# The loads of two weight matrices move from the ScalarE and SyncE queues to GpSimd's queue

## The chip, the cores and the metric

The kernel runs on one core of one Trainium2 chip. Time is device time of that core in microseconds (us); a time of the kernel is the median of several runs. The core has TensorE (PE, with its weight loads shown as PEld), VectorE (DVE), ScalarE (ACT), GpSimd (POOL) and SyncE (SP). Each engine runs its own program in order. A DMA command stands in the program of an engine like any other instruction: if it has to wait for a free buffer, what stands behind it on that engine waits too.

## The reference

Block-sparse attention (4 batches, 8 heads, 768 positions, head size 64, blocks of 32) and, on its output, two matrix products with a nonlinearity between them:

```python
scores = scale * q @ k.T                       # per batch and head, masked to a window of 3 blocks,
attn = softmax(where(mask, scores, -1e9))      # 2 global blocks and 3 sampled blocks per row of blocks;
x = (attn @ v) as [3072, 512]                  # first and last row of blocks are dense
h = x @ w_in                                   # w_in  [512, 2048]
g = h * tanh(softplus(h))
out = g @ w_out                                # w_out [2048, 512]
```

## The kernel before

**Staging.** The inputs q, k, v are scaled and split into two half-precision parts, and so are the two weight matrices, so that each product is three half-precision products. Attention runs in jobs: each batch has 13, eleven with two rows of blocks and two dense ones. A job is scores (S, line 661), a maximum on VectorE, exponentials on ScalarE, transposes (T, line 667), the product with v (O, line 789), a normalisation and one more transpose (tx). The second part runs in stages of 256 positions, three to a batch (0, 1, 2): first product h (line 1049, in runs of 12 matmuls), copies hs, elementwise us and g on three engines, second product y (line 1114, in runs of 6 matmuls). The names h_1_5 and y_0_0 give the stage and then the piece of h (0 to 7) or the half of y.

**Weights.** w_in comes in 8 pieces of 1 MB (tile wr, 3 buffers), w_out in 16 pieces of 512 KB (tile wor, in the ring of 6 buffers "raw" that q, k and v use as well). A piece is a wide number; VectorE decodes it in three steps (lines 873, 876, 879). TensorE then forms a Gram matrix of each (gram_wi, gram_wo), from whose diagonal comes one scale: tp_wo (line 387) is the matmul that sums the diagonal for the whole of w_out, so it needs all 16 decoded pieces. After it each piece of w_out is scaled (wt_o, line 965 or 963), rounded (line 969 or 968) and the rest subtracted on GpSimd (line 970). A run of y for two pieces needs those two.

**GpSimd's other work.** The gathers of sampled key blocks (lines 567 and 598, three copies for a row of blocks, six for a job; a few of the first jobs may run on ScalarE), which write one of two buffers kg and so wait for the scores of an earlier job; the low halves of some inputs (lines 507, 522), squares (line 1083) and the low half of g (line 1099).

**What sets the order.** All work is entered as tasks with an engine (or a choice of engines), a duration, what it reads and writes, and a key. A planner, Plan.emit, simulates the engines, picks the task that can start first by its durations (keys and the tables URGE, JOBS and PIECES decide between near ones), and writes the programs in that order. One duration or engine that changes can thus move any task behind it. Where the simulation sees a gap on TensorE between 14 and 200 us of its own time, `fill` writes dummy matmuls into it (line 1309, one for each 0.14 us of the gap; they write an unused part of a bank). Work on the second part is taken when nothing of attention is ready, with the earliest piece first; four buffers g hold its results, so h can run at most about two stages ahead of y.

Of the kernel before, what the change touches and what calls it, by code (L numbers as in the profile page):

```python
# [37 lines left out]
def place(w):  # L38

    name, *at = w[0] if w and isinstance(w[0], tuple) else (None,)  # L40
    if name in ("s", "mx", "nb", "p", "t", "ph", "pl", "o", "r", "tx", "xhw", "xw"):
        return (name, at[0], None) if at[0] < len(JOBS) else (None, None, None)
    if name in ("wr", "wi", "wq", "ws", "wor", "wo"):
        return name, None, at[0] + 8 * (name in ("wor", "wo"))
    if name in ("wd", "wh", "wl", "wt", "dg") and at[0] in ("i", "o") and len(at) > 1:
        return name + at[0], None, at[1] + 8 * (at[0] == "o")
    if name == "gram" and at[0] == "wi":
        return "gram", None, at[1]
    if name in ("raw", "ss", "sc", "hi", "tp", "gram", "ends") and len(at) > 1 and at[1] == 0 or \
            name in ("k", "q", "v", "vd", "kt") and at[0] == 0:  # L50
        return name + str(at[0] if name in ("raw", "ss", "sc", "hi", "tp", "gram", "ends") else ""), None, None
    return (name if name in ("us", "hs", "gh", "gp", "hsw", "kg", "kw", "vg", "ys", "iv", "am") else None), None, None
# [12 lines left out]
class Plan:  # L65
# [10 lines left out]
    def add(self, eng, dur, fn, r=(), w=(), new=(), use=(), key=0.0, lat=0.0, kind=None, port=False, also=()):  # L76

        kind_, i, k = place(w)  # L80
        key += URGE.get(kind_, 0.0) + (JOBS[i] if i is not None else 0.0) + (PIECES[k] if k is not None else 0.0)
        t = Task({eng: (dur, fn, port or (eng == "POOL" and dur)), **{e: (d, f, o) for e, d, f, o in also}}, key, lat,
                 new, kind, len(self.tasks))
        self.tasks.append(t)
        for ring, k in new:
            self.first[k], self.users[k] = t, []
        for k in r:
            t.deps.update(self.writer.get(k, ()))
            self.readers.setdefault(k, []).append(t)
        for k in w:  # L90
            t.deps.update(self.writer.get(k, ()))
            t.deps.update(self.readers.pop(k, ()))
            self.writer[k] = [t]
        for k in {*r, *w, *use}:
            if k in self.users:
                self.users[k].append(t)
                t.deps.add(self.first[k])
        t.deps.discard(t)
        return t
# [109 lines left out]
def attn_mish_kernel(ctx: ExitStack, tc: tile.TileContext, qT, kT, v, sampled, blocks, w_in, w_out, out):  # L209
# [11 lines left out]
    nc = tc.nc  # L221
# [20 lines left out]
    wide = w_in.dtype != F32  # L242
# [12 lines left out]
    wo = const.tile([P, NFC, 2, DM], F16, name="wo")  # L255
# [72 lines left out]
    BOTH = True  # L328
# [3 lines left out]
    add = plan.add  # L332
# [525 lines left out]
    def load_w(pool, key, tag, w, a0, eng):  # L858

        if not wide:  # L860
            eng.dma_start(out=a0, in_=w)
            return
        n = w.free_size()
        raw = new(pool, tag, key, [P, RAW if tag == "raw" else n])[:, 0:n].bitcast(I32)
        eng.dma_start(out=raw.rearrange("p (c f) -> p c f", c=w.shape[1]) if len(w.shape) == 3 else raw, in_=w)
        tl[key] = raw.rearrange("p (f two) -> p f two", two=2)
# [18 lines left out]
    def a0_i(k):  # L885
        return wi[:, k].rearrange("p m t c f -> p (m t c f)").bitcast(F32)

    def load_i(k):
        W = 2 if wide else 1
        src = w_in.rearrange("(c p) f -> p c f", p=P)[:, :, k * 2 * P * W:(k + 1) * 2 * P * W]  # L890
        key, raw = ("wi", k), ("wr", k)

        after = [("raw", "v", 0, 1)]
        if wide:
            go = lambda eng: load_w(pools["w"], raw, "wr", src, None, eng)
            add("ACT", 0.45, lambda: go(nc.scalar), r=after, w=[raw], new=[("wr", raw)], key=-9, lat=2.0,
                kind=("dma", 3.9), also=[("SP", 0.5, lambda: go(nc.sync), False)] if BOTH else ())
            return
        add("ACT", 0.45, lambda: load_w(None, None, None, src, a0_i(k).rearrange("p (c f) -> p c f", c=NCC),
                                          nc.scalar), r=after,  # L900
            w=[key], key=-9, lat=2.0, kind=("dma", 1.95))

    def piece_i(k, cls):

        k0 = k - k % 2
        key, ks, ksc, kp = ("wi", k), ("wq", k0), ("ws", k0), ("tp", "w", k0)
        load_i(k)
        add_decode(("wr", k), key, lambda: a0_i(k), 1.24, cls)

        def ss():  # L910
            if k == k0:
                new(sb, "wq", ks, [P, 2])
            return tl[ks][:, k - k0:k - k0 + 1]
        add_gram(("wi", k), [lambda: a0_i(k)], [key], "h", ss, [ks], [("wq", ks)] if k == k0 else (), cls)
        if k > k0:

            add_root(kp, lambda: tl[ks], lambda: root(kp, new(sb, "ws", ksc, [P, 2]), iv_i[:, k0:k + 1]),
                     [ks], [], [ksc, ("iv", k0)], [("ws", ksc)], cls, apart=True)
            split_i(k0, cls)
            split_i(k, cls)  # L920
# [59 lines left out]
    def a0_o(fc):  # L980
        return wo[:, fc].rearrange("p t d -> p (t d)").bitcast(F32)

    def load_o(fc, after=()):
        raw = ("wor", fc)
        go = lambda eng: load_w(sb, raw, "raw", w_out.rearrange("(c p) f -> p c f", p=P)[:, fc], a0_o(fc), eng)
        add("ACT", 0.45, lambda: go(nc.scalar), r=after, w=[raw] + ([] if wide else [("wo", fc)]), new=[("raw", raw)],
            key=-5, lat=2.0, kind=("dma", 1.95), also=[("SP", 0.5, lambda: go(nc.sync), False)] if BOTH else ())

    def piece_o(fc, cls):

# [182 lines left out]
    for j in T3:  # L1173
        load(0, "v", [j], "us" if j < 2 else "hs")
    add("ACT", 1.0, lambda: which(new), w=["off", "z"],
        new=[("hs", ("z",))], key=-9, lat=6.0)
# [21 lines left out]
    for k in range(NFP):  # L1198
# [3 lines left out]
        key=-9)  # L1202
# [23 lines left out]
    for i, job in enumerate(jobs):  # L1226
# [19 lines left out]
        if i == 1:  # L1246
            LOADO, ATO, ATP = [("dec", 6)], -2.0, -22.0
            for fc in range(NFC):
                load_o(fc, after=LOADO)
                piece_o(fc, ATO)  # L1250
            scale_o(ATO)
            for fc in range(NFC):
                parts_o(fc, ATP)
# [104 lines left out]
```

## Time and profile before

| | |
|---|---|
| median of 3 runs | 789.8 us (788.79 to 790.77) |
| span of the profiled execution, first to last instruction | 786.6 us (the page gives no other time for it; 3.2 under the median) |
| TensorE busy | 740.5 us |
| ScalarE, VectorE, GpSimd busy | 542.7, 493.5, 307.6 us |
| mean granted TensorE clock | 0.990 |
| DMA moved | 95.31 MB, mean 121 GB/s |

In the rows of the profile an engine's work is given as line, engine, operation, output<-input, shape and count, with start and duration or with busy time and mean. "[6.40 <-DMA vg<-vd]" behind a row says that the engine stood idle for 6.40 us before it and what ended that, inferred from semaphores. ACTq, SPq and POOLq are an engine's commands that are not counted as busy, the DMA commands among them. A row with "x8: 374/374/520, 10.5 to 50.9" gives the count, the shortest, median and longest duration in ns, and the start of the first and last.

### The profile page before, as it was taken

Reading aid. Unit: us, or ns where it says so; the run is one execution under the profiler, and the core shown is the slowest. Engines: PE = TensorE matmul, PEld = TensorE weight load, DVE = VectorE, ACT = ScalarE, POOL = GpSimd, SP = SyncE. Lnnn points to the kernel's source line nnn. Section 1 sums busy time; section 2 is a strip of 40 time slices with the busy share of each in tenths; the row PEclk is TensorE's granted clock in tenths of the full one; section 3 lists DMA queues with packets and bytes.
Section 4 is the critical chain, followed back from the end, with each engine's and each line's share of the span. In section 5 each row is a group of like instructions: output and inputs, shape, how many; then the busy total and the mean of one; then the engine's idle time right before and its main releaser. Section 6 shows DMA issues by size and latency. Waiting matters only on the chain.

```text
span 786.6 us, 30628 instructions
## 1 busy us (share of the span) xinstructions
PE 740.5 (94%) x12793; PEld 518.7 (66%) x12793; DVE 493.5 (63%) x900; ACT 542.7 (69%) x880; POOL 307.6 (39%) x393
## 2 busy tenths in 40 slices
PE   6677899888999999999999999999999999999997
PEld 5544578665577767767776676677677667666663
DVE  6868988998767764795866457656665453223220
ACT  3555778768868877777887768786876666455650
POOL 2114244887635542374443422534641331213021
PEclk9989999999999999999999999999999999999999
DMA  9878857104534475244346603523444112000000
GB/s 339 263 236 256 268 176 202 44 2 136 159 117 131 119 198 171 69 162 120 87 139 194 192 15 101 174 77 91 119 115 119 37 39 81 14 15 14 14 14 27
DMA packets 57742, 95.31 MB, mean 121 GB/s; under 512 B 8323, under 2 KB 20612, under 8 KB 57604
## 3 DMA queue, kind: packets, MB, share of 16 engines
q1 hardware_dynamic: 52032, 80.51, 34.9%
q10 hardware_dynamic: 5572, 12.85, 4.8%
q8 instruction: 100, 1.64, 0.9%
q14 instruction: 38, 0.31, 0.1%
HBM read 80.38 MB, written 12.95 MB: 119 GB/s over the span
## 4 chain that ended last, share of the span: by engine, by line
PE 73%; DVE 10%; ACT 6%; DMA 5%; issue 2%; POOL 1%; SPq 1%; POOLq 1%; ACTq 0%; DVEq 0%
PE h_None L1049 27%; PE y L1114 26%; PE obank L789 6%; PE t L667 6%; PE s L661 4%; DMA vg<-vd 3%; PE tx L667 1%; PE wd_i L947 1%; DVE wt_o L965 1%; DMA wr<-in_moe_w_in_dram 1%; DVE hs_None L1087 1%; DVE v L491 1%; DMA raw_k<-in_k_dram 1%; ACT us_None L1078 1%; POOL kt L522 1%
## 5 line engine op out<-in xcount | busy, mean ns | idle before, releaser
L1049 PE MATMUL h_None<-xh,wi 128*128 128x256 f16 x1536 | 282.8, 273 | 0.0
L1114 PE MATMUL y<-wo,g 128*128 128x512 f16 x1152 | 278.0, 380 | 4.0 <-POOL wo L970 2.6
L1049 PEld LDWEIGHTS <-wi 128*128 128x128 f16 x2304 | 223.5, 98 | 47.3 <-issue 2.1
L1049 PE MATMUL h_None<-xl,wi 128*128 128x256 f16 x768 | 209.8, 273 | 0.0
L1114 PEld LDWEIGHTS <-g 128*128 128x128 f16 x1152 | 111.1, 98 | 106.7 <-issue 7.3
L1099 POOL TENSOR_TENSOR g<-hs_None,g 128x1024 f16<-128x1024 f32 x48 | 107.6, 2241 | 188.4 <-DVE g L1096 144.8
L598 POOL COPY kg<-kt 128x256 f16 x258 | 107.2, 451 | 123.3 <-PE s L661 109.7
L1060 ACT ACTIVATE hs_None<-h_None,gsc 128x512 f32<-128x512 f32 x96 | 65.5, 684 | 80.2 <-PE h_None L1049 79.4
L727 ACT ACTIVATE pt<-s,nb,ns 128x256 f32<-128x256 f32 (+1 forms) x208 | 106.3, 582 | 5.7 <-PE t L667 5.0
L750 ACT ACTIVATE ph<-t 128x512 f16<-128x512 f32 x112 | 66.5, 596 | 45.1 <-PE t L667 45.0
L754 DVE SCALAR_TENSOR_TENSOR pl<-t,ph 128x512 f16<-128x512 f32 x105 | 71.9, 686 | 35.8 <-ACT ph L750 35.5
L1087 DVE SCALAR_TENSOR_TENSOR hs_None<-us_None,hs_None 128x1024 f32<-128x1024 f32 x48 | 65.0, 1355 | 40.1 <-ACT us_None L1086 40.1
L667 PE MATMUL t<-ident,pt 128*128 128x128 f32 x448 | 70.4, 280 | 6.8 <-DVE pl L754 3.6
L708 DVE TENSOR_REDUCE mx<-s 128x4 f32<-128x1024 f32 x44 | 53.7, 1222 | 31.9 <-PE s L661 31.3
L1083 POOL TENSOR_TENSOR us_None<-us_None 128x1024 f32<-128x1024 f32 x22 | 44.2, 2007 | 71.8 <-DVE us_None L1081 68.7
L667 PEld LDWEIGHTS t<-ident,pt 128*128 128x128 f32 x448 | 51.6, 142 | 21.4 <-DVE pl L754 4.5
L789 PEld LDWEIGHTS <-ph 128*32 128x32 f16 x3584 | 47.9, 94 | 20.9 <-issue 13.1
L1078 ACT ACTIVATE us_None<-hs_None,hsc 128x1024 f32<-128x1024 f32 x48 | 55.2, 1150 | 0.9
L789 PE MATMUL obank<-vg,ph 128*32 128x65 f16 (+1 forms) x3200 | 50.6, 196 | 4.0 <-DMA vg<-vd 2.2
L1081 DVE TENSOR_SCALAR us_None<-us_None 128x1024 f32<-128x1024 f32 x48 | 37.4, 778 | 25.4 <-ACT us_None L1078 25.2
L1085 ACT ACTIVATE us_None<-us_None 128x1024 f32<-128x1024 f32 x48 | 50.7, 1056 | 1.6 <-POOL us_None L1083 0.8
L1086 ACT ACTIVATE us_None<-us_None 128x1024 f32<-128x1024 f32 x48 | 50.7, 1056 | 0.8
(199 smaller groups left out, 893.6 us busy)
## 6 DMA issues: line engine op xcount, KB each, us to landing
vg<-vd SPq DMA_DIRECT2D x320, 65.0 KB, 2.6
vg<-vd SPq DMA_DIRECT2D x80, 195.0 KB, 3.2
wr<-in_moe_w_in_dram ACTq DMA_DIRECT2D x8, 1024.0 KB, 7.4
vd<-v SPq DMA_DIRECT2D x12, 520.0 KB, 3.8
vg<-vd SPq DMA_DIRECT2D x12, 520.0 KB, 5.1
raw_k<-in_k_dram SPq DMA_DIRECT2D x12, 512.0 KB, 5.4
raw_q<-in_q_dram SPq DMA_DIRECT2D x12, 512.0 KB, 4.3
raw_v<-in_v_dram SPq DMA_DIRECT2D x12, 512.0 KB, 5.0
```

What stands on the lines that cost most here:

```text
L598: nc.gpsimd.tensor_copy(out=dst, in_=tl["kt", b][:, :, ds(j, BS)])
L667: nc.tensor.matmul(out, src, ident, start=start, stop=stop, is_transpose=True)
L727: ex = lambda o, x, g, w: nc.scalar.activation(out=o, in_=x, func=AF.Exp, bias=nb[:, g, w:w + 1], scale=tl["ns", b, sus[w]["qb"] // TB][:, ...
L750: nc.scalar.activation(out=new(sb, "ph", ("ph", i, j), [P, 2, 2, P], F16), in_=tl["t", i, j], func=AF.Copy, scale=PSC)
L754: nc.vector.scalar_tensor_tensor(out=new(sb, "pl", ("pl", i, j), [P, 2, 2, P], F16), in0=tl["t", i, j], scalar=PSC, in1=tl["ph", i, j], op ...
L789: nc.tensor.matmul(o[cs, w, g, 0:v1 - v0], p[:, k, g, cs], vt[:, k, 2 * c + g, v0:v1], start=j == 0 and g == 0 and k == 0 and n == 0, stop ...
L1049: nc.tensor.matmul(h[:, f2, 0:n].rearrange("p (s q) -> p s q", q=BS), wi[:, fp, cc // 2, w, cc % 2, fs], x[:, s0:s0 + sn, cc], start=f2 == ...
L1060: nc.scalar.activation(out=tl[kq][:, 2 * (fp % 2):2 * (fp % 2) + 2, 0:n], in_=tl[kh][:, :, 0:n], func=AF.Copy, scale=gsc[:, fp:fp + 1])
L1078: nc.scalar.activation(out=us(), in_=hs(), func=AF.Exp, scale=hsc[:, b:b + 1])
L1087: add("DVE", 1.32 * c, lambda: nc.vector.scalar_tensor_tensor(out=hs(), in0=us(), scalar=-0.5, in1=hs(), op0=ALU.add, op1=ALU.mult), r=[ku ...
L1099: add("POOL", 2.3 * c, lambda: nc.gpsimd.tensor_tensor(out=g(1), in0=hs(), in1=g(0), op=ALU.subtract), r=[kq, ("gh",) + kp], w=[kp], use=[kg])
L1114: nc.tensor.matmul(tl[ky], tl["g", b, t, k][:, g, f, q], wo[:, fc, w], start=fc == 0 and n == 0, stop=fc == NFC - 1 and n == 2)
```

## The change

The loads of w_in and w_out are entered as tasks of GpSimd with a duration of 1.0 us in place of ScalarE's with 0.45 us, and without the choice of SyncE. (With "POOL" and a duration, the planner also counts the port that GpSimd shares with VectorE as held for that time.) Nothing else in the source differs.

```diff
         if wide:
             go = lambda eng: load_w(pools["w"], raw, "wr", src, None, eng)
-            add("ACT", 0.45, lambda: go(nc.scalar), r=after, w=[raw], new=[("wr", raw)], key=-9, lat=2.0,
-                kind=("dma", 3.9), also=[("SP", 0.5, lambda: go(nc.sync), False)] if BOTH else ())
+            add("POOL", 1.0, lambda: go(nc.gpsimd), r=after, w=[raw], new=[("wr", raw)], key=-9, lat=2.0,
+                kind=("dma", 3.9))
             return
...
         go = lambda eng: load_w(sb, raw, "raw", w_out.rearrange("(c p) f -> p c f", p=P)[:, fc], a0_o(fc), eng)
-        add("ACT", 0.45, lambda: go(nc.scalar), r=after, w=[raw] + ([] if wide else [("wo", fc)]), new=[("raw", raw)],
-            key=-5, lat=2.0, kind=("dma", 1.95), also=[("SP", 0.5, lambda: go(nc.sync), False)] if BOTH else ())
+        add("POOL", 1.0, lambda: go(nc.gpsimd), r=after, w=[raw] + ([] if wide else [("wo", fc)]), new=[("raw", raw)],
+            key=-5, lat=2.0, kind=("dma", 1.95))
```

Since the planner works from these durations, the programs of all engines come out in another order. Three places show what that means.

ScalarE early in the program, before the change: casts of pieces of w_in (wd_i, line 951), with loads of later pieces (wr) between them.

```order
L727 ACTIVATE pt_1204<-s_1008,nb_1202,ns_0_270 128x256 x2
L865 DMA wr_1258<-in_moe_w_in_dram 128x4x512
L951 ACTIVATE wi<-wd_i_0_1255 128x512
L865 DMA wr_1374<-in_moe_w_in_dram 128x4x512
L951 ACTIVATE wi<-wd_i_1_1260 128x512
L750 ACTIVATE ph_0_1379<-t_0_1246 128x512
```

ScalarE at the same casts, with the change.

```order
L727 ACTIVATE pt_1185<-s_821,nb_1060,ns_0_270 128x256 x2
L951 ACTIVATE wi<-wd_i_0_1183 128x512
L727 ACTIVATE pt_1185<-s_821,nb_1060,ns_0_270 128x256 x2
L763 ACTIVATE pl_2_1215<-t_2_1094 128x512
L951 ACTIVATE wi<-wd_i_1_1190 128x512
L750 ACTIVATE ph_0_1336<-t_0_1198 128x512
```

The loads are gone from between the casts. ScalarE's program has no load of a weight any more, and neither has SyncE's.

GpSimd where the elementwise work of the second part begins, before the change: behind the last gather of the first ten jobs with two rows of blocks.

```order
L598 COPY kg_111<-kt_228 128x8x32
L1083 TENSOR_TENSOR us_0_1_None<-us_0_1_None 128x1024
L1099 TENSOR_TENSOR g_0_0_4414<-hs_0_0_None,g_0_0_4414 128x1024
L1083 TENSOR_TENSOR us_0_2_None<-us_0_2_None 128x1024
L970 TENSOR_TENSOR wo<-wt_o_4618,wo 128x512
L970 TENSOR_TENSOR wo<-wt_o_4621,wo 128x512
L1099 TENSOR_TENSOR g_0_1_4713<-hs_0_1_None,g_0_1_4713 128x1024
```

GpSimd at the same place with the change; wor_4330 is the 16th and last piece of w_out.

```order
L598 COPY kg_111<-kt_228 128x8x32
L1099 TENSOR_TENSOR g_0_0_4244<-hs_0_0_None,g_0_0_4244 128x1024
L865 DMA wor_4330<-in_moe_w_out_dram 128x1024
L1083 TENSOR_TENSOR us_0_2_None<-us_0_2_None 128x1024
L1099 TENSOR_TENSOR g_0_1_4593<-hs_0_1_None,g_0_1_4593 128x1024
L1099 TENSOR_TENSOR g_0_2_4615<-hs_0_2_None,g_0_2_4615 128x1024
L1099 TENSOR_TENSOR g_0_3_4754<-hs_0_3_None,g_0_3_4754 128x1024
L1083 TENSOR_TENSOR us_1_1_None<-us_1_1_None 128x1024
L970 TENSOR_TENSOR wo<-wt_o_4910,wo 128x512
L970 TENSOR_TENSOR wo<-wt_o_4914,wo 128x512
```

The last load stands where the first splits of w_out stood, and these stand behind three more subtracts of g. The five loads ahead of it lie one by one behind the gathers of earlier jobs. Before, all 16 subtracts of line 970 follow within 46 rows of GpSimd's program, with 6 copies of gathers among them; with the change nine do, and seven come later, behind three subtracts of the next batch's k (line 522) and among 24 copies of gathers in all.

TensorE where the diagonal of all of w_out is summed, before the change.

```order
L1049 LDWEIGHTS wi
L1049 MATMUL h_0_6_None<-xh_0_1475,wi 128x256
L387 MATMUL tp_wo<-am_wo,ones 128x1
L1049 LDWEIGHTS wi
L1049 MATMUL h_0_6_None<-xh_0_1475,wi 128x256
```

TensorE at the same matmul, with the change.

```order
L1049 LDWEIGHTS wi
L1049 MATMUL h_1_5_None<-xh_1_3051,wi 128x256
L387 MATMUL tp_wo<-am_wo,ones 128x1
L1049 LDWEIGHTS wi
L1049 MATMUL h_1_6_None<-xh_1_3051,wi 128x256
```

The sum stands behind 28 runs of h instead of 13. The dummy matmuls of line 1309 are 253 with the change and 109 before; 122 of them lie behind tp_wo among the eight runs of y_0_0, where the order of before has none.

## The prediction, made before the changed kernel ran

> **What bounds the kernel now.** I read the page's first part, then the windows by stage, then who waited for whom on TensorE, then the timelines of the places the change touches. In the windows the columns are busy time (and instructions) of PE, PEld, DVE, ACT and POOL, then the granted clock, the DMA share and GB/s.
>
> ```profile
> span 786.6 us, 30628 instructions
> PE 740.5 (94%) x12793; PEld 518.7 (66%) x12793; DVE 493.5 (63%) x900; ACT 542.7 (69%) x880; POOL 307.6 (39%) x393
> 0.00:100.00 100.00, 74.29 (x1555) 50.98 (x1556) 77.89 (x176) 57.07 (x111) 24.52 (x50) 0.95 0.85 273
> 100.00:135.00 35.00, 33.74 (x958) 28.37 (x957) 29.37 (x57) 28.36 (x55) 17.43 (x26) 1.00 0.62 176
> 135.00:187.30 52.30, 44.54 (x539) 32.16 (x537) 48.67 (x68) 40.66 (x59) 39.94 (x30) 0.97 0.20 62
> 187.30:786.60 599.30, 587.92 (x9747) 407.19 (x9745) 337.60 (x601) 416.59 (x659) 225.75 (x287) 1.00 0.34 98
> ```
>
> TensorE is busy 740.5 of 786.6 us, and 34.7 us of what it lacks lie ahead of 187.3 us (25.7 in the first 100, 1.3 up to 135, 7.8 up to 187.3). Behind that it misses 11.4 in 599. So the kernel is TensorE's own instructions plus the waits of the first 187 us, and a change of the loads is worth what it does to two things there: the waits, and the dummy matmuls that the planner writes into gaps that it sees (L1309). Those run in line; where TensorE has other work to do they cost their full time.
>
> ```profile
> PE wd_i L956 <- ACT wi L951: 5.5, 1, 5.5
> PE t L667 <- DVE pl L754: 3.6, 1, 3.6
> PE y L1114 <- POOL wo L970: 2.6, 3, 0.9
> PE wd_i L947 <- ACT wi L951: 1.8, 1, 1.8
> PE t L667 <- ACT pt L727: 1.2, 1, 1.2
> ```
>
> These are the waits ahead of 200 us that the change can reach: ScalarE's casts of w_in, the transposes behind VectorE and ScalarE, and the second product y behind GpSimd's pieces of w_out.
>
> **The change, part by part.** The 24 loads leave ScalarE (16) and SyncE (8) and stand in GpSimd's program. The planner then writes a new order for every engine, and that order is the larger part.
>
> *Dummy matmuls.* The order has 253 of them instead of 109: 125 instead of 109 ahead of the first h, 6 more ahead of tp_wo, 122 behind tp_wo, among y_0_0, where the order of before has none.
>
> ```profile
> L1309 PE MATMUL obank<-neg 128*128 128x240 f16 x109 | 15.6, 282 | 3.8 <-DVE xs L811 3.8
> 18.53 3.75 PE L1309 MATMUL obank<-neg 128*128 128x240 f16 x35
> ```
>
> The longest run gives 3.75 / 35 = 0.107 us each, the mean over all is 15.6 / 109 = 0.143, which holds the runs on a slow clock. The new ones stand in long runs, so I take 0.107: 144 x 0.107 = **+15.4 us** (upper end 20.6).
>
> *ScalarE's queue without loads.*
>
> ```profile
> 48.68 0.38 ACTq L865 DMA_DIRECT2D wr<-in_moe_w_in_dram  x1
> 49.10 0.60 ACT L951 ACTIVATE wi<-wd_i 128x512 f16<-128x512 f32 x1 [6.40 <-DMA vg<-vd]
> ```
>
> ScalarE stood 6.40 us ahead of a cast of w_in, because the load in front of it in the same queue waited until 48.68 us; TensorE lost the 5.5 us of the first row above by it. Without the load in that queue the cast goes when its matmul is done. What is late next is the same w_in piece, whose load now waits in GpSimd's queue for the same buffer and holds the gathers behind it. Between 0 and -5.5 I take **-3**.
>
> *When w_out arrives.* By the rows below the 16 loads were issued between 60.4 and 105.3 us by two engines, landed in 7.9 us (ScalarE's median), and the last of three decode steps began at 130.1.
>
> ```profile
> L865 ACTq DMA_DIRECT2D wor<-in_moe_w_out_dram x8: 334/366/710, 60.4 to 89.3; - x8
> L865 SPq DMA_DIRECT2D wor<-in_moe_w_out_dram x8: 328/362/852, 82.8 to 105.3; - x8
> L879 DVE SCALAR_TENSOR_TENSOR wo<-wor,wo x16: 674/685/1203, 67.1 to 130.1; 128x512 int32<-128x512 int32 x16
> wor<-in_moe_w_out_dram ACTq DMA_DIRECT2D x8, 512.0 KB, 7.9
> 122.43 1.10 POOL L598 COPY kg<-kt 128x256 f16 x2 [0.26 <-POOL kg L598]
> 130.72 2.59 POOL L1099 TENSOR_TENSOR g<-hs_None,g 128x1024 f16<-128x1024 f32 x1
> ```
>
> In the new order the last six loads stand one by one behind the gathers of a job, the 16th behind 57 copies (60 with ScalarE's three, as many as the 54 and 6 of before, which ended at 123.5) and behind the subtract of g_0_0, which ended at 133.3. With landing (7.9) and three decode steps of at most 0.7 the weights are whole at about 143, against 131 before. Is that too late? TensorE reads it at tp_wo, at 135.06 before.
>
> ```profile
> 135.06 0.28 PE L387 MATMUL tp_wo<-am_wo,ones 128*128 128x1 f32 x2
> 104.52 1.31 PE h_None L1049 x12
> 143.00 1.46 PE L1114 MATMUL y<-wo,g 128*128 128x512 f16 x6
> 185.80 1.47 PE L1114 MATMUL y<-wo,g 128*128 128x512 f16 x6
> ```
>
> In the new program tp_wo stands behind 28 runs of h (12 matmuls, 1.31 us) instead of 13, behind 22 more dummies (2.4) and some 1.5 us of attention: 135.1 + 19.7 + 2.4 + 1.5 - 3 = 155.7. The late weights are hidden there with 12.7 us to spare; TensorE's own order, not the transfer, puts the splits of w_out 20 us later. The runs of h are no loss, only work done early.
>
> *The stretch from tp_wo to the end of the eighth y run.* Before: 135.06 to 187.27, 52.2 us with 7.8 of waits. In the new order it holds 4 runs of h instead of 18, 8 runs of y, 122 dummies, and 384 score, 62 transpose and 480 output matmuls of attention instead of 192, 22 and 48. The next rows are TensorE in 200 to 300 us for the transposes (L667), the outputs (L789) and the scores (L661).
>
> ```profile
> 200.00:300.00 100.00, 16.75 (x101) 11.58 (x102) 1.00 0.54 153
> 200.00:300.00 100.00, 11.68 (x1104) 10.27 (x1104) 1.00 0.54 153
> 200.00:300.00 100.00, 8.81 (x480) 5.70 (x480) 1.00 0.54 153
> ```
>
> So 4 x 1.31 + 8 x 1.29 (a y run is 1.46 with its tail and is followed at 1.29) + 122 x 0.107 + 62 x 0.166 + 480 x 0.0106 + 384 x 0.0184 = 5.2 + 10.3 + 13.1 + 10.3 + 5.1 + 7.1 = 51.1 us of instructions. GpSimd's path through the same stretch is longer: its last seven pieces of w_out come behind three subtracts of the next batch's k, and 24 copies of gathers lie among the 16 pieces.
>
> ```profile
> L970 POOL TENSOR_TENSOR wo<-wt_o,wo x16: 1155/1328/2137, 140.1 to 181.8; 128x512 f16<-128x512 f32 x16
> 119.56 0.40 POOL L598 COPY kg<-kt 128x256 f16 x1 [0.18 <-PE s L661]
> 120.26 0.40 POOL L598 COPY kg<-kt 128x256 f16 x1 [0.31 <-POOL kg L598]
> 185.10 2.14 POOL L522 TENSOR_TENSOR kt<-raw_k,kt 128x1024 f16<-128x1024 f32 x1 [1.76 <-DVE kt L518]
> 157.41 1.29 POOL L507 TENSOR_SCALAR raw_k<-raw_k,sc_k 128x1024 f32<-128x1024 f32 x1
> 128.87 1.90 POOL L1083 TENSOR_TENSOR us_None<-us_None 128x1024 f32<-128x1024 f32 x1 [5.34 <-DVE us_None L1081]
> ```
>
> 5.0 from tp_wo to the first piece (135.06 to 140.1) + 16 x 1.33 + 24 x 0.70 (0.40 and the 0.30 between starts) + 3 x 2.14 + 2 x 1.29 + 1.90 + 1.3 for the last y = 55.3; with copies at 0.40 it is 48.1. So the stretch lasts 51 (no wait beside the dummies) to 55 and more, since each gather also waits for the scores of the job before. Waits of 7.8, as before, would make it 59. I take **0** as the change of the waits; ends: -7.8 (none is left) and +9, the 2.6 + 3.6 + 1.2 + 1.8 of the rows above a second time.
>
> *Transfers.* The bytes and DMA engines are the same, and SyncE's eight commands (0.36 each) were not on the path. By the Trainium skill, *DMA: Bandwidth & Descriptors*, section "Issuing engines are not separate DMA queues", all issuing engines end on the same 16 DMA engines, and a second issuer saves only sequencer time. By that rule alone the loads would cost 24 x 0.37 us on GpSimd instead of elsewhere and the time would not move; the trace agrees as far as both queues' 512 KB loads land in the same order of time.
>
> **Sum** against the profiled execution: 15.4 - 3 + 0 = +12.4 on a span of 786.6, so 799.0. The median of the runs shown is 3.2 us above that span: 802.
>
> **Rivals.**
> 1. *Not slower: ScalarE's relief pays for the dummies.* Place: ScalarE's queue up to 100 us. All of the 5.5 goes, the 1.8 and 1.2 behind ScalarE too, and the 7.8 between 135 and 187 because y comes later than its weights: 15.4 - 5.5 - 3.0 - 7.8 = -0.9, about 789. It decides if the stretch behind tp_wo has no wait left, that is if GpSimd ends its pieces in less than 51 us. For it: the 6.40 row. Against: GpSimd's 55.
> 2. *GpSimd's loads are held by VectorE, and w_out becomes the wait.* GpSimd's pieces take 1155 ns at best, 2137 at worst, beside VectorE. If each of the 16 loads is held for one decode step of 1.22 us (rows below), the weights come 19.5 us later, 12.7 are free, and tp_wo waits 6.8: 809. With the longest row of VectorE near there, 3.14, it is 16 x 3.14 - 12.7 = 38 more, 840.
>
> ```profile
> L876 DVE SCALAR_TENSOR_TENSOR wi<-wr,wi x8: 1216/1222/1307, 20.7 to 63.3; 128x1024 int32<-128x1024 int32 x8
> 143.12 3.14 DVE L1087 SCALAR_TENSOR_TENSOR hs_None<-us_None,hs_None 128x1024 f32<-128x1024 f32 x1
> ```
>
> The Trainium skill, *SBUF — State Buffer*, section "SBUF: two separate sides", speaks against this change: a load from GpSimd's queue has its descriptors written by GpSimd, which is locked out while VectorE runs in a two-port mode; it gives 620 ns alone and 3100 beside such a copy. An estimate by it, 16 x 2.5 less the 12.7, is +27. No run so far shows a load on GpSimd.
> 3. *Nothing moves*, since the transfers are hidden and the order's gaps are real: the dummies only fill time that was idle. 790.
>
> **How the numbers follow.** Forecast 0.72, rival 1 0.09, rival 2 0.14, rival 3 0.05. The predicted time is the forecast's, 802. Its own ends are 15.4 - 5.5 - 7.8 = +2.1 (792) and 20.6 + 9 = +29.6 (819); the range is 790 to 822: it takes in rival 3 and the nearer part of rival 2, and leaves out rival 1 (0.09) and rival 2 beyond 822 (0.06). A measurement of this kernel can tell about 0.3% (2.4 us). Faster: 0.05, from rival 1. Same: 0.10, from rivals 1 and 3 and the forecast's low end. Slower: 0.85.
>
> **What would show it.** 253 dummies at about 0.107 us, 27 us in all; ScalarE without the 6.40 us idle ahead of L951; tp_wo near 156 us; TensorE waiting for pieces of w_out (L970) and for exponentials between 156 and 215; the eighth y run ending near 215; behind it TensorE as full as before. Wrong would be: tp_wo waiting for its weights (rival 2), TensorE busy throughout behind tp_wo (rival 1), or new waits later than 230 us, which nothing here prices.

## The result and the profile after

The changed kernel takes 809.8 us (median of four runs, 805.5 to 812.0) against 789.3 (four runs, 788.6 to 790.8): a ratio of 1.0259, interval 1.0223 to 1.0294, so 20.5 us or 2.6% slower. The forecast was 802 in a range of 790 to 822: the direction and the range hold, the size was forecast as 12.4 and came out as 20.5. The profiled execution took 810.73 us.

The page of the changed kernel, its first lines:

```profile
span 809.0 us, 30926 instructions
PE 755.6 (93%) x12937; PEld 534.0 (66%) x12937; DVE 479.2 (59%) x896; ACT 551.6 (68%) x887; POOL 309.6 (38%) x414
```

From its groups by line, the dummy matmuls:

```profile
L1309 PE MATMUL obank<-neg 128*128 128x240 f16 x253 | 31.9, 277 | 4.1 <-DVE xs L811 4.1
```

The span grew by 22.4 us: TensorE's busy time by 15.1 (740.5 to 755.6; the dummies alone make 16.3, 31.9 against 15.6), its idle time by 7.3 (46.1 to 53.4). On the face of it that is the forecast's sum with a second term for waits. To see where the time lies I cut both traces at the same three events: the first matmul of h, tp_wo, and the end of the eighth run of y. The columns are those of the windows shown in the prediction. The kernel before:

```profile
0.00:102.59 102.59, 76.86 (x1618) 52.62 (x1619) 80.34 (x181) 59.09 (x116) 25.98 (x54) 0.95 0.84 272
102.59:135.06 32.47, 31.23 (x904) 26.80 (x895) 26.98 (x52) 26.40 (x49) 15.97 (x23) 1.00 0.62 173
135.06:187.27 52.21, 44.45 (x538) 32.07 (x537) 48.61 (x68) 40.57 (x59) 39.94 (x30) 0.97 0.20 61
187.27:786.60 599.33, 587.95 (x9747) 407.22 (x9745) 337.60 (x601) 416.62 (x659) 225.75 (x287) 1.00 0.34 98
```

The changed kernel:

```profile
0.00:100.32 100.32, 74.91 (x1615) 52.24 (x1615) 74.19 (x171) 56.42 (x110) 39.60 (x74) 0.98 0.82 257
100.32:162.38 62.06, 56.16 (x1155) 47.97 (x1154) 44.98 (x77) 49.45 (x79) 24.34 (x31) 0.97 0.50 150
162.38:225.18 62.80, 52.55 (x1162) 38.72 (x1161) 51.07 (x101) 50.23 (x87) 43.98 (x55) 0.97 0.36 108
225.18:809.00 583.82, 571.98 (x9010) 395.04 (x9008) 308.92 (x548) 395.47 (x613) 201.70 (x255) 1.00 0.32 92
```

| stage | TensorE idle before | after |
|---|---|---|
| up to the first h | 25.7 | 25.4 |
| to tp_wo | 1.2 | 5.9 |
| to the end of the eighth y run | 7.8 | 10.3 |
| to the end | 11.4 | 11.8 |

The last stage waits no more than before. The stretch from tp_wo to the eighth y run lasts 62.8 us instead of the 51 to 55 worked out, and tp_wo comes at 162.38 instead of 155.7. TensorE's waits in the changed kernel (waited for, us in total, times, longest), up to 100 us:

```profile
PE gram_q L361 <- DMA raw_q<-in_q_dram: 4.6, 1, 4.6
PE gram_v L361 <- DMA raw_v<-in_v_dram: 2.1, 3, 1.8
```

From 100 to 162 us:

```profile
PE obank L789 <- issue: 3.1, 2, 1.9
...
PE gram_wo L361 <- DVE wo L879: 0.2, 1, 0.2
```

From 162 to 225 us:

```profile
PE obank L1309 <- DVE xs L811: 3.5, 2, 2.7
PE y L1114 <- POOL wo L970: 2.0, 2, 1.8
PE t L667 <- DVE pl L754: 1.6, 3, 0.6
```

The 5.5 us for wd_i behind ScalarE are gone. New are the waits for q (4.6 instead of 1.8) and v (2.1 instead of nothing) at the very start, a stage that the prediction left alone. And although TensorE shows only 10.3 us of waits behind tp_wo, 15.7 us of its busy time there are dummies. The window of the stretch for line 1309 alone (PE, PEld, clock, DMA share, GB/s):

```profile
162.38:225.18 62.80, 15.74 (x122) 12.72 (x122) 0.97 0.36 108
```

Idle time and dummies together, TensorE has no work of its own for 26.0 us of this stretch, against 7.8 before.

### The profile page after: what moved, and what is told of

It is laid out like the page before. It is cut to its first block, busy times and chain, and to the rows that moved or that the text cites. A ratio compares the mean times of both kernels' runs of the same rounds, so it can differ in the third digit from the quotient of the medians.

```text
span 809.0 us, 30926 instructions
## 1 busy us (share of the span) xinstructions
PE 755.6 (93%) x12937; PEld 534.0 (66%) x12937; DVE 479.2 (59%) x896; ACT 551.6 (68%) x887; POOL 309.6 (38%) x414
## 4 chain that ended last, share of the span: by engine, by line
PE 78%; DVE 8%; DMA 6%; issue 3%; ACT 3%; SPq 1%; POOL 0%; DVEq 0%; POOLq 0%; ACTq 0%
PE h_None L1049 28%; PE y L1114 28%; PE t L667 6%; PE obank L789 5%; PE s L661 5%; DMA vg<-vd 2%; DMA raw_q<-in_q_dram 2%; DMA raw_v<-in_v_dram 2%; PE obank L1309 1%; PE wd_i L947 1%; DVE hs_None L1087 1%; PE tx L667 1%; DMA raw_k<-in_k_dram 1%; DVE wt_o L965 1%; DVE pl L754 1%
## 5 line engine op out<-in xcount | busy, mean ns | idle before, releaser
L598 POOL COPY kg<-kt 128x256 f16 x261 | 109.6, 453 | 104.1 <-PE s L661 89.8
L1087 DVE SCALAR_TENSOR_TENSOR hs_None<-us_None,hs_None 128x1024 f32<-128x1024 f32 x48 | 62.8, 1309 | 48.6 <-ACT us_None L1086 47.8
L1083 POOL TENSOR_TENSOR us_None<-us_None 128x1024 f32<-128x1024 f32 x18 | 35.5, 1974 | 49.4 <-DVE us_None L1081 46.4
L789 PE MATMUL obank<-vg,pl 128*32 128x65 f16 x1600 | 47.6, 194 | 1.5 <-issue 1.5
```

Source lines behind the costliest of these rows:

```text
L598: nc.gpsimd.tensor_copy(out=dst, in_=tl["kt", b][:, :, ds(j, BS)])
L789: nc.tensor.matmul(o[cs, w, g, 0:v1 - v0], p[:, k, g, cs], vt[:, k, 2 * c + g, v0:v1], start=j == 0 and g == 0 and k == 0 and n == 0, stop ...
L1087: add("DVE", 1.32 * c, lambda: nc.vector.scalar_tensor_tensor(out=hs(), in0=us(), scalar=-0.5, in1=hs(), op0=ALU.add, op1=ALU.mult), r=[ku ...
```

## The experiments

Twelve kernels ran, in four groups on four chips. The kernel before ran beside each group: 789.4 us with runs 1 to 4, 786.1 with 5 to 8, 790.0 with 9 to 11, 789.3 with 12. I therefore compare ratios to it; 0.1% is 0.8 us.

| run | us | ratio | interval |
|---|---|---|---|
| changed kernel | 809.8 | 1.0259 | 1.0223 to 1.0294 |
| 1 no late dummies | 808.7 | 1.0259 | 1.0197 to 1.0320 |
| 2 old order, GpSimd issues | 792.8 | 1.0061 | 1.0031 to 1.0091 |
| 3 new order, SyncE issues | 802.5 | 1.0174 | 1.0111 to 1.0237 |
| 4 only w_out moved | 819.0 | 1.0347 | 1.0267 to 1.0427 |
| 5 new order, GpSimd, loads behind v | 803.3 | 1.0213 | 1.0176 to 1.0250 |
| 6 old order, GpSimd, loads behind v | 787.9 | 1.0018 | 0.9998 to 1.0038 |
| 7 no subtract of pieces | 805.9 | 1.0246 | 1.0208 to 1.0283 |
| 8 planned anew for SyncE | 802.0 | 1.0155 | 1.0101 to 1.0208 |
| 9 narrow split | 810.2 | 1.0269 | 1.0231 to 1.0307 |
| 10 old order, five of w_in by GpSimd | 788.3 | 0.9990 | 0.9964 to 1.0016 |
| 11 old order, five of w_in by SyncE | 789.2 | 0.9990 | 0.9968 to 1.0013 |
| 12 narrow split, no late dummies | 803.5 | 1.0179 | 1.0115 to 1.0243 |

**Run 1: do the dummies stand in line?**

```diff
-    FILL = 14.0, 200.0
+    FILL = 14.0, 100.0
```

> The changed kernel without the 128 dummy matmuls behind its first h (the window in which the planner may write them ends at 100 us instead of 200; order and everything else stay). Theory (the dummies stand in line on TensorE and cost about their own time, and the waits of the new order cost the rest): 128 x 0.107 = 13.7 us less, of which up to 4 come back as waits of y for GpSimd's pieces of w_out, so 796 to 800 against 810. Rival (the dummies lie in gaps that the new order has anyhow): 807 to 812, with the 13.7 us as idle time behind tp_wo.

It took 808.7 us, the same ratio as the changed kernel. The theory falls. The window of the stretch behind tp_wo without its 122 dummies:

```profile
160.65:223.75 63.10, 46.02 (x1040) 29.41 (x1039) 51.10 (x101) 50.17 (x87) 43.82 (x55) 0.84 0.36 107
```

What TensorE waits for in it (160 to 225 us):

```profile
PE t L667 <- DVE pl L754: 4.3, 5, 2.1
PE y L1114 <- POOL wo L970: 3.0, 2, 2.7
PE tx L667 <- DVE xl L839: 1.9, 1, 1.9
PE y L1114 <- DVE wo L969: 1.6, 1, 1.6
```

The stretch lasts 63.1 us with no dummies and 62.8 with 122 of them. The dummies' time came back as 6.8 us of idle time (10.3 to 17.1) and as slower matmuls: the granted clock fell from 0.97 to 0.84, and the instructions other than dummies took 46.0 us instead of 37 to 39 (52.55 less the 15.74 of the row above, or less 122 x 0.107). So leaving the dummies out gains nothing that this run can tell; its interval leaves room for some 5 us.

That does not make every dummy a filler of idle time. The changed kernel has one place where they stand in the way. The dummies write a part of obank, and by the trace a run of them waited until VectorE (L811) had read that bank (two rows of the timeline, then a window with the columns of before):

```profile
202.90 4.39 PE L1309 MATMUL obank<-neg 128*128 128x240 f16 x25 [2.70 <-DVE xs L811]
207.55 0.38 PE L667 MATMUL tx<-ident,xs 128*128 128x128 f32 x2
202.90:207.20 4.30, 4.30 (x26) 3.36 (x26) 0.76 (x2) 1.15 (x2) 1.15 (x1) 0.60 0.94 311
```

The gap that they were to fill was TensorE's own wait for xs, so it has passed when these 25 start. Then they take 4.3 us at a granted clock of 0.60, and the transpose tx, for which xs was ready, stands behind them. In run 1 the same transpose follows xs at once, while a run of y later in the stretch takes 2.72 us instead of 1.46:

```profile
203.48 0.41 PE L667 MATMUL tx<-ident,xs 128*128 128x128 f32 x2 [0.31 <-DVE xs L811]
211.19 2.72 PE L1114 MATMUL y<-wo,g 128*128 128x512 f16 x6
```

The traced chain that ends last goes through dummies for 13.1% of the changed kernel's stretch (8.2 us). In run 1 it goes through GpSimd's pieces of w_out (L970, 11.4%) and its subtracts of the next k (L522, 10.1%), and the stretch is as long. What the dummies would cost at an equal clock no run here shows. Counting an instruction's time in a busy column is not the same as knowing what is gained without it.

**Runs 2 and 3: the order and the queue taken apart.** The planner decides the order from what it is told; the queue is which engine issues the command. Run 2 tells the planner what the kernel before told it and issues from GpSimd; run 3 tells it what the changed kernel tells it and issues from SyncE. The loads of w_in are shown; those of w_out are edited alike.

```diff
-            add("ACT", 0.45, lambda: go(nc.scalar), r=after, w=[raw], new=[("wr", raw)], key=-9, lat=2.0,
-                kind=("dma", 3.9), also=[("SP", 0.5, lambda: go(nc.sync), False)] if BOTH else ())
+            add("ACT", 0.45, lambda: go(nc.gpsimd), r=after, w=[raw], new=[("wr", raw)], key=-9, lat=2.0,
+                kind=("dma", 3.9), also=[("SP", 0.5, lambda: go(nc.gpsimd), False)] if BOTH else ())
```

> The kernel before with its order kept on every engine, but the 24 load commands issued by GpSimd at the places at which the planner had put those of ScalarE and SyncE. Theory (the queue itself is worth nothing or less than nothing, the new order costs everything): 786 to 792, and ScalarE's 6.40 us ahead of L951 gone. Rival (GpSimd's queue costs: its commands take 0.5 to 0.75 us each, stand among its gathers and hold them): 796 or more, with waits for kg copies or for decoded weights that the kernel before does not have.

```diff
-            add("POOL", 1.0, lambda: go(nc.gpsimd), r=after, w=[raw], new=[("wr", raw)], key=-9, lat=2.0,
+            add("POOL", 1.0, lambda: go(nc.sync), r=after, w=[raw], new=[("wr", raw)], key=-9, lat=2.0,
```

> The changed kernel with its order kept on every engine, but the 24 load commands issued by SyncE at the same places in the written order. Theory (the new order costs): 805 to 812, no change against the changed kernel. Rival (GpSimd's queue costs the 7 us of new waits): 799 to 804, with the 5.9 us of idle time between the first h and tp_wo back near 1.2.

Run 2: 0.6% slower than before (2.4 to 7.2 us), a little outside the theory's 786 to 792 and short of the rival's 796. Run 3: 1.7% slower, at the rival's number, not the theory's. So most of the loss is the order's, but not all of it. The rival named the wrong place, though. Run 3's first two stages:

```profile
0.00:97.11 97.11, 77.38 (x1615) 54.43 (x1616) 75.18 (x171) 56.78 (x110) 27.10 (x55) 0.95 0.85 263
97.11:158.66 61.55, 56.30 (x1156) 47.97 (x1154) 45.66 (x79) 49.65 (x79) 22.04 (x26) 0.97 0.52 155
```

Between the first h and tp_wo it idles 5.3 us, as the changed kernel does (5.9), not the 1.2 of before. What can be put down to the queue lies ahead of the first h, which comes 3.2 us earlier: 19.7 us idle instead of 25.4. (Another 5.4 us of the two traces' difference lie behind the eighth y run, where the same instructions took from 578.4 us in run 3 to 583.8 in the changed kernel; one execution of each does not tell that from chance.) The cause shows where TensorE sums the squares of v (L361; the columns are lowest, median and highest ns, then first and last start). The kernel before:

```profile
L361 PE MATMUL gram_v<-raw_v x24: 268/308/308, 11.7 to 14.2; 128*128 128x128 bf16 x24
```

Its load commands of w_in:

```profile
L865 ACTq DMA_DIRECT2D wr<-in_moe_w_in_dram x8: 374/374/520, 10.5 to 50.9; - x8
```

The sums of v in the changed kernel:

```profile
L361 PE MATMUL gram_v<-raw_v x24: 286/308/312, 18.9 to 22.1; 128*128 128x128 bf16 x24
```

Its load commands:

```profile
L865 POOL DMA_DIRECT2D wr<-in_moe_w_in_dram x8: 748/750/983, 2.4 to 56.0; - x8
L865 POOL DMA_DIRECT2D wor<-in_moe_w_out_dram x16: 528/530/602, 67.1 to 134.6; - x16
```

ScalarE issued its first load of w_in at 10.5 us. GpSimd has nothing to do at the start and issues three, 1 MB each, from 2.37 us, ahead of v's own loads on SyncE. The timelines of the two (start, duration):

```profile
2.37 2.49 POOL L865 DMA_DIRECT2D wr<-in_moe_w_in_dram  x3
```

```profile
4.90 3.81 SPq L419 DMA_DIRECT2D raw_v<-in_v_dram  x3
```

From 10 to 20 us the DMA engines move 399 GB/s before and 400 in the changed kernel; TensorE, which was busy for 9.55 of these 10 us, is busy for 3.17. Its window there:

```profile
10.00:20.00 10.00, 3.17 (x20) 2.47 (x20) 3.54 (x12) 4.37 (x4) 0.00 (x0) 1.00 1.03 400
```

So v is 7 us later. The planner's condition that w_in comes behind v sets the order in its list; on the chip no engine waits for it.

**Run 4: w_out alone.** Against the changed kernel, the loads of w_in go back.

```diff
-            add("POOL", 1.0, lambda: go(nc.gpsimd), r=after, w=[raw], new=[("wr", raw)], key=-9, lat=2.0,
-                kind=("dma", 3.9))
+            add("ACT", 0.45, lambda: go(nc.scalar), r=after, w=[raw], new=[("wr", raw)], key=-9, lat=2.0,
+                kind=("dma", 3.9), also=[("SP", 0.5, lambda: go(nc.sync), False)] if BOTH else ())
```

> Only the 16 loads of w_out go to GpSimd's queue; those of w_in stay where they were. The planner's order for it has 223 dummies, 114 more than before: 98 ahead of the first h, 31 up to tp_wo, 94 behind it. Theory (dummies in line): 114 x 0.107 = 12.2 us, and up to 7 of waits, so 801 to 809. Rival (the early loads of w_in, which now compete with k, q and v at the start, or GpSimd's waits for their buffers, cost it): 789 to 793.

It is slower than both theories said, 819. Its first h is early (94.69 us) and its eighth y run ends at 208.5; the loss lies behind:

```profile
208.50:300.00 91.50, 84.62 (x1656) 58.08 (x1656) 57.99 (x107) 70.15 (x120) 41.24 (x60) 0.98 0.40 114
300.00:400.00 100.00, 94.24 (x1563) 66.71 (x1563) 58.39 (x108) 68.90 (x106) 31.39 (x36) 0.97 0.44 126
```

TensorE idles 12.6 us from 208.5 to 400, where the changed kernel loses 4.9 from 225 to 400. TensorE's largest wait there is for transfers of v (vg), 5.0 us in three. That order is worse in places that neither theory speaks of; why was not followed up. It refutes the rival: the order made for w_out's loads alone is enough to lose time.

**Runs 5 and 6: is it the early issue?** A copy of one column of v on GpSimd ahead of each of the first three loads makes GpSimd wait until v has landed, in the new order (5) and in the old (6).

```diff
+            if k < 3:
+                nc.gpsimd.tensor_copy(out=gox, in_=tl["flat", "v", 0, 1][:, 0:1])
             load_w(pools["w"], raw, "wr", src, None, eng)
```

> The changed kernel, with a copy of one column of v by GpSimd ahead of each of the first three loads of w_in, so that GpSimd issues them only when v has landed and not at 2.4 us, ahead of v's own loads. Theory (the whole part of the loss that went with SyncE's queue in the third run is the early issue, which takes bandwidth from v): the sums of squares of v (L361) begin near 12 us instead of 18.9, and the time is 800 to 804. Rival (it is GpSimd's commands among its gathers): 807 to 812, with the waits for v gone and others in their place.

> The kernel before with its order kept, the 24 commands issued by GpSimd as in the second run, and the copy of a column of v ahead of the first three. Theory (without the early issue GpSimd's queue only takes the 6.40 us stall off ScalarE): 782 to 787 against 789. Rival (GpSimd's commands cost as much as the stall was worth): 788 to 793.

The sums of v in run 5:

```profile
L361 PE MATMUL gram_v<-raw_v x24: 268/308/308, 12.1 to 14.5; 128*128 128x128 bf16 x24
```

Its loads of w_in:

```profile
L865 POOL DMA_DIRECT2D wr<-in_moe_w_in_dram x8: 748/748/983, 12.2 to 51.1; - x8
```

Its first stage:

```profile
0.00:95.51 95.51, 77.65 (x1614) 53.80 (x1615) 73.52 (x171) 56.23 (x110) 42.37 (x77) 0.96 0.86 270
```

The sums begin at 12.1 and the first h at 95.5 instead of 100.3: theory, 803.3 us. By ratios the early issue costs 2.59 - 2.13 = 0.46% in the new order and 0.61 - 0.18 = 0.43% in the old (run 2 to run 6), 3.4 to 3.6 us; first h comes 4.8 and 4.5 us earlier (in run 2 at 108.30, in run 6 at 103.81). The intervals of run 5 and the changed kernel overlap; the size rests on two pairs and two traces that agree. Run 3 (1.0174) and run 5 (1.0213) start their loads of w_in at nearly the same time (13.2 and 12.2 us) and differ in the issuing engine; their intervals overlap, so a cost of GpSimd's commands in the new order is neither shown nor excluded.

Run 6 is the reverse of the change's other half: GpSimd issues all 24, the order is that of before, nothing is early, and the kernel is no slower and no faster (1.0018, 0.9998 to 1.0038). So in the old order GpSimd's queue as such costs nothing measurable. The theory had asked for 782 to 787, since ScalarE's stall is gone too; the rival's 788 to 793 was as near. TensorE's waits in run 6 up to 110 us show what came in place of the 5.5:

```profile
PE obank L789 <- issue: 7.0, 3, 3.4
PE gram_q L361 <- DMA raw_q<-in_q_dram: 4.2, 1, 4.2
```

Against 2.9 and 1.8 before, these take back 4.1 + 2.4 us.

**Runs 10 and 11: the stall alone.** The old order again; the first three loads of w_in stay with ScalarE, the other five go to GpSimd (10) or SyncE (11).

```diff
-            add("ACT", 0.45, lambda: go(nc.scalar), r=after, w=[raw], new=[("wr", raw)], key=-9, lat=2.0,
+            add("ACT", 0.45, lambda: go(nc.scalar if k < 3 else nc.gpsimd), r=after, w=[raw], new=[("wr", raw)], key=-9,
+                lat=2.0,
```

> The kernel before with its order kept; of its eight loads of w_in the first three stay with ScalarE and the other five are issued by GpSimd at the same places; w_out's stay where they were. Theory (only the 6.40 us stall of ScalarE goes, and v's loads meet nothing new): TensorE's 5.5 us for wd_i are gone, 782 to 786 against 786 to 789 of the kernel before. Rival (the load now holds GpSimd's gathers while it waits for its buffer, and TensorE waits for them): no difference, 786 to 791.

> As the run before, but the five later loads of w_in are issued by SyncE. Theory (only the stall of ScalarE goes): 782 to 786. Rival (SyncE, waiting for a buffer of w_in, holds the gathers of v that it issues): 787 to 792, with TensorE waiting for vg.

Both give 0.999 with 1 in the interval. This was meant to beat both kernels and does not. The first stage of run 10:

```profile
0.00:102.85 102.85, 80.19 (x1619) 56.16 (x1619) 79.96 (x181) 59.27 (x116) 30.26 (x59) 0.90 0.85 270
```

Of TensorE's waits for wd_i behind ScalarE 0.4 us is left in it, idle time fell from 25.7 to 22.7 us, and yet the first h comes at 102.85 (102.59 before): the clock granted was 0.90 instead of 0.95, and the same 1619 matmuls took 3.3 us longer. In run 11 the clock stayed at 0.95 and first h came at 102.34; of the waits for wd_i 1.1 us is left, and the idle time is 25.3 us as before, with other waits in their place. Both times lie where the rivals had them, but TensorE shows no wait for gathers of k in run 10 and none for vg in run 11, as the rivals had it. The stall of ScalarE was a wait, but not one that the rest of the stage hung on.

**Runs 7, 9 and 12: what makes the stretch 63 us long?**

```diff
-            add("POOL", 1.2, lambda: nc.gpsimd.tensor_tensor(out=lo, in0=tl[kt], in1=hi, op=ALU.subtract),
+            add("POOL", 1.2, lambda: nc.gpsimd.memset(lo, 0.0) if key[0] == "o" else
+                nc.gpsimd.tensor_tensor(out=lo, in0=tl[kt], in1=hi, op=ALU.subtract),
```

> The changed kernel with GpSimd's 16 subtracts of w_out (L970, 1155 to 2137 ns) replaced by 16 memsets of the same tiles, so the low halves of w_out are left out of the product; the order stays. Theory (GpSimd's path sets the stretch from tp_wo to the end of the eighth y run, 62.8 us): the stretch falls to 55 or less, and the time to 798 to 803. Rival (the chain of attention jobs on VectorE and ScalarE, busy for 51 and 50 of the 62.8 us, sets it): the stretch stays at 60 or more, the time at 806 to 812.

Of the next edit, run 9's, one of ScalarE's lines is shown; VectorE's and the casts are cut to the same 64 columns.

```diff
+            n = 64 if key[0] == "o" else 512
-                    nc.scalar.activation(out=t, in_=a0(), func=AF.Copy, scale=sc())
+                    nc.scalar.activation(out=t[:, 0:n], in_=a0()[:, 0:n], func=AF.Copy, scale=sc())
```

> The changed kernel with the split of w_out cut down: ScalarE and VectorE scale and cast 64 of each piece's 512 columns (L963, L965, L968, L969: 0.71, 0.74, 0.63 and 0.42 us before), and GpSimd writes zeros instead of the subtract (two memsets, about 0.69 each, so as long as it was busy before). Seven eighths of w_out's columns and all its low halves are left out of the product. Theory (ScalarE and VectorE, busy for 50 and 51 of the 62.8 us, set the stretch from tp_wo to the end of the eighth y run; some 8 us go from each): the stretch falls to 50 to 57, the time to 797 to 804. Rival (the attention jobs' chain of scores, maxima, exponentials, transposes and outputs sets it): the stretch stays at 59 or more, the time at 805 to 811.

> The first and the ninth run together: the changed kernel without the 128 dummies behind its first h and with the split of w_out cut down (seven eighths of its columns and all its low halves left out of the product). In the first run the stretch from tp_wo to the end of the eighth y run lasted 63 us without dummies, in the ninth about 61 with dummies and almost no split. Theory (two chains of nearly one length run beside each other there, TensorE's instructions with the dummies and the pieces of w_out with the attention jobs, so that neither edit alone shows): the stretch falls to 48 to 56, the time to 794 to 802. Rival (the attention jobs and the preparation of the next k, q and v alone set it): 59 or more, 803 to 810.

The stretch of each, in this order (7, 9, 12):

```profile
160.71:220.30 59.59, 50.89 (x1162) 37.95 (x1161) 47.99 (x101) 49.78 (x88) 33.38 (x55) 1.00 0.37 115
```

```profile
164.50:225.95 61.45, 53.66 (x1162) 39.42 (x1161) 45.32 (x102) 44.91 (x88) 36.05 (x71) 0.94 0.36 111
```

```profile
160.95:218.30 57.35, 43.82 (x1040) 28.81 (x1039) 46.02 (x101) 44.43 (x87) 35.42 (x70) 0.88 0.38 119
```

Taking 10.6 us of work off GpSimd shortens the stretch by 3.2; taking 5.8 off VectorE, 5.3 off ScalarE and 7.9 off GpSimd (whose memsets came out shorter than supposed) shortens it by 1.4; leaving out the dummies alone, by nothing. With the changed kernel's instructions untouched the stretch lasted 61.7 to 62.8 us (run 5, run 3, the changed kernel), so run 9's 1.4 is hardly beyond chance; the granted clock differs as well (1.00, 0.94 and 0.88 in the three rows), and by their ratios runs 7 and 9 are no faster than the changed kernel. Both theories of a single engine fall. The two edits together shorten it by 5.5, which neither does alone. That fits two chains of nearly one length, TensorE's with its dummies and that of w_out's pieces, but does not prove them: run 12's 57.35 lies between its theory's 56 and its rival's 59, and its 803.5 us at the lower end of the rival's range. What is left then, 57 us without dummies and with little of the split, is attention jobs and the next batch's k, q and v. No one engine was shown to set that.

**Run 8: any other order?** All 24 loads on SyncE, the planner told so (0.5 us, no hold on the port).

```diff
-            add("POOL", 1.0, lambda: go(nc.gpsimd), r=after, w=[raw], new=[("wr", raw)], key=-9, lat=2.0,
+            add("SP", 0.5, lambda: go(nc.sync), r=after, w=[raw], new=[("wr", raw)], key=-9, lat=2.0,
```

> All 24 loads on SyncE, and the planner is told so (0.5 us each on SyncE, no hold on the port that GpSimd and VectorE share in its model). It makes an order of its own with 216 dummies, 90 of them behind tp_wo, and 24 runs of h ahead of tp_wo instead of 13. Theory (what costs is that a new order was made, in which the runs of h are spent ahead of tp_wo; GpSimd has no part in it): 797 to 808. Rival (the order is bad because the planner is told 1.0 us on GpSimd with the port held): 787 to 793.

1.0155: the time is the theory's. The loads of w_out are edited alike. An order made for SyncE, with 216 dummies and 20 runs of h ahead of tp_wo (the expectation miscounted them as 24), loses 12 us without GpSimd issuing a load. The theory's reason is not shown by it: its first h comes at 113.46 us, and its stretch lasts 63.5 us although 12 runs of h are left in it, while run 4's order has 7 left and a stretch of 51.0. GpSimd's price of 1.0 us is not needed to get a worse order: of three new orders (this, run 4's and the changed kernel's) none came near the old one.

## Why the prediction was right, and where it was not

*The size.* By the ratios the 20.4 us are made up of 15.4 for the order (run 5 to run 6, 2.13 - 0.18 = 1.95%), 3.6 for the early loads, and 1.4 (-0.2 to 3.0) for GpSimd's queue with ScalarE's stall gone. Forecast were 15.4, nothing, and -3. So the mis-sized terms are the last two, 3.6 and 4.4 us off: **ScalarE's -3 was worth nothing that can be measured**, and **the change of waits, taken as 0**, was 3.6 at a place for which the prediction had no row: it asked when w_out arrives, and did not ask when GpSimd would issue w_in. By the intervals these sizes carry some 3, 3 to 4 and 1.6 us of uncertainty.

*The dummies.* Their number and place were right, and their busy time nearly (16.3 us more than before, where 15.4 was taken). The sentence "Those run in line; where TensorE has other work to do they cost their full time" did not carry over to the kernel's time: run 1 leaves out 128 of the 144 and gains nothing that can be told, although in the changed kernel some 8 us of them lie on the traced chain. That the order costs 15.4 and the dummies were priced at 15.4 is therefore luck as far as these runs show. Rival 3 was right that the order's gaps are real, and wrong that nothing moves: the gaps are new, 26.0 us of the stretch without work of TensorE's own instead of 7.8. The runs of h that filled TensorE's time behind tp_wo (18 of them) had been used up ahead of it (4 were left), and attention jobs, each waiting for VectorE and ScalarE between its matmuls, stand in their place. "The runs of h are no loss, only work done early" is, on this reading, the step that failed: work done early is no longer there as cover. The counts and the gaps are from the traces; that the one makes the other is argued. Runs 4 and 8 show that the number of h runs left does not set the length of the stretch by itself.

*The stretch, 51 to 55.* 62.8. Both bounds summed instructions of one engine, TensorE 51.1 and GpSimd 55.3. GpSimd's own work did not set it: it waited itself (the waits of the changed kernel's GpSimd from 162 to 225 us), and run 7 took 10.6 us of its work away for 3.2.

```profile
POOL wo L970 <- DVE wo L969: 11.3, 5, 4.2
POOL kg L598 <- PE s L661: 4.0, 2, 3.6
```

*tp_wo at 155.7.* 162.38. The 28 runs of h are there. TensorE's instructions ahead of tp_wo came to 23.0 us more than before, near the 23.6 worked out (19.7 + 2.4 + 1.5). What was wrong is the idle time: 3 us were taken off, and it grew by 4.3 (26.97 to 31.31), all of it between the first h and tp_wo (1.2 to 5.9).

*Transfers hidden.* Right: TensorE waited 0.5 us for decoded pieces of w_out (0.3 ahead of 100 us, 0.2 behind). **Rival 2** is out: the commands of the 16 loads of w_out took GpSimd 528 to 602 ns and the 8 of w_in 748 to 983, with VectorE busy beside most of them, and tp_wo did not wait for its weights. The Trainium skill, *SBUF — State Buffer*, section "SBUF: two separate sides", gives about 3100 ns for a transfer from GpSimd's queue beside a VectorE copy that locks the shared port. None of the 24 commands took a third of that; whether one of them met a VectorE instruction that takes that lock, the runs do not show. **Rival 1** is out by the result, and runs 6, 10 and 11 show that ScalarE's relief is worth nothing measurable.

*Behind the eighth y run.* Right: 11.8 us idle against 11.4. It ended at 225.2, not 215, for the reasons above.

*The rule on issuing engines.* The Trainium skill, *DMA: Bandwidth & Descriptors*, section "Issuing engines are not separate DMA queues": run 6, in the old order, agrees, with no difference that can be measured. What I did not draw from it: where transfers share the engines, an issuer that is free earlier takes bandwidth earlier. Here v came 7 us later at an unchanged 400 GB/s.

## What to carry to other kernels

Before a filler instruction is priced, ask whether the engine has anything else to do at that place, and what the filler itself has to wait for; leave it out in one run, and read the granted clock with the time, since both change. Work that is moved ahead of a wait can be missing as cover behind it, so compare what stands beside the waiting chain, not sums of one engine. When a load moves to another queue, look at what that engine does at that moment: an idle one issues at once, and an order that only the old engine's lateness gave has to be made by a real dependence.

## What the runs showed of the hardware

With the 122 dummies in the stretch the granted clock was 0.97 (changed kernel), 1.00 (run 7) and 0.94 (run 9); without them it was 0.84 (run 1) and 0.88 (run 12). Up to the first h (102 to 108 us) the clock was 0.90 (run 10), 0.91 (run 2) and 0.95 (before, run 11) for the same matmuls in the same order, worth 3 to 5 us of TensorE's busy time; what decides it stays open. A load command took GpSimd 0.53 us (512 KB) or 0.75 us (1 MB) of its own time in the changed kernel (medians), where in the kernel before ScalarE and SyncE took some 0.37.
